# A fused retention layer and channel-mix layer: two blocks in 64-token chunks, and a new order of all pieces

## Chip, cores and metric

The kernel runs on one core of one Trainium2 chip. The metric is device microseconds of one launch. The time before is 153.07 us, the median of three runs (153.02 to 153.23).

## What is computed

```python
# attention: q, k, v of shape (4, 8, 768, 64); per head a decay gamma
for t in range(S):
    state = gamma * state + outer(k[t], v[t])       # 64 x 64
    y[t] = q[t] @ state / sqrt(D)
x = y.transpose(0, 2, 1, 3).reshape(4, 768, 512)
# channel mix: d_model 512, d_ff 1024
x_prev = x shifted by one token (zero first)
xk = mu_k * x + (1 - mu_k) * x_prev
xr = mu_r * x + (1 - mu_r) * x_prev
k = maximum(xk @ w_k, 0);  v = (k * k) @ w_v
out = sigmoid(xr @ w_r) * v
```

The output is float32; the kernel multiplies in float16 and sums in float32.

## The kernel before

The 4 x 768 tokens are cut into 12 blocks of 256 tokens; blocks 0 to 2 are the first sequence, 3 to 5 the second, and so on. The recurrence is done in chunks: inside a chunk by masked scores (queries times keys) times values, across chunks by a state of 64 x 64 per head, with the decay folded into scale factors of v and of the result. A block is done in one of three forms. Blocks 0 and 1 use chunks of 128 tokens made of even and odd tokens. Blocks in `WIDE` (2 to 5) use two plain chunks of 128 tokens with score tiles of 128 x 128. Blocks in `HALF` (6 to 11) use four chunks of 64 tokens with score tiles of 64 x 64, so that TensorE works on four 64x64 tiles; these have more, smaller matmuls and one mask instruction instead of two, but four running states instead of two. The transposes of blocks 0 to 3 (`WHOLE`) read 128 rows, those of the others 64.

Nothing is scheduled automatically. `ORDER` is a text that lists every piece of the program; the loop at its end issues the pieces in that order, each to the engine behind the `~` (v VectorE, a ScalarE, p GpSimd's queue, s SyncE's queue; none is TensorE), with the PSUM banks behind the `@`. Each engine works through its own queue strictly in this order; semaphores for the data are set automatically. The codes, with the block as the first number:

- `lq`, `lk`, `lv`: loads of q, k, v (float32 in memory; q and k land as float16); `wk`, `wr`, `wv`: weights. Their issues stand in GpSimd's queue (lines 230, 235, 735, 738, 742).
- `Tq`, `Tk`: transposes (272, 278); `Eq`, `Ek`: their copies to `qT`, `kT` on ScalarE (241).
- `vs`: scaling of v (253), mostly VectorE, for blocks 1 and 3 GpSimd.
- `S`: scores (318 in the 64-token form, 331 wide, 339 the first form); `M`: mask (347, 354).
- `C`: state of the chunk (366 in the 64-token form, 384, 395); `U`: running state sums (419); `G`: decay to the next block, on ScalarE 4 instructions (424).
- `I`, `J`: state times queries (441); `Y`: masked scores times values (462 in the 64-token form, 478 wide, 489), in the 64-token form with `J` inside it.
- `D`: scaled result to `xT` (507, 514); `dx`: difference of neighbouring tokens (529); `t`: the same role for block 0 on ScalarE (542); `X.n.0.j`, `X.n.1.j`: mixed inputs xk and xr of block n, column chunk j of four (552, 558).
- `K`: xk @ w_k (582; 572 for pairs of blocks that share a group); `Qa`, `Qb`: relu and square on ScalarE (591, 599, 603); `R`: xr @ w_r (612); `s`: its sigmoid (618); `V`: times w_v (624; `Vc` in halves 642); `O`: product (630, 649); `st`: store (637).
- `z`: matmuls of zeros (703, 710), which fill TensorE's waiting time at the start.

The dense pieces `K`, `R`, `V` need all column chunks of the mixed inputs of their group; a group is one block or a pair (`GROUPS`: 3 with 4, 6 with 7, 9 with 10).

Of the kernel before, what the change touches and what calls it, by code (L numbers as in the profile page):

```python
# [48 lines left out]
X.3.1.2~v I.6@01 J.5 X.3.1.0~v D.5~v X.3.1.1~v Qb.3.3~a G.6~a V.2.1.0@2 K.3.1@3 V.2.1.1 O.2.1~v  # L49
Qb.3.7~a Qa.3.1~a Qb.3.1~a dx.5~v K.3.4@4 K.3.5@5 Qa.3.5~a X.5.0.0~v X.5.0.3~v R.3.1@2 s.3.1~a  # L50
lv.7~p Qa.3.4~a X.5.0.1~v Qb.3.4~a R.3.0@5 R.4.0@2 s.3.0~a s.4.0~a Qb.3.0~a X.5.0.2~v vs.7~v K.5.2@4
S.7@67 st.1.1~s M.7~v Qb.3.5~a Y.6 Qb.3.6~a lv.10~p C.7@23 U.7.0~v X.5.1.1~v Qa.5.2~a K.5.0@5
R.4.1@6 Qa.5.0~a D.6~v s.4.1~a V.4.0.0@4 V.4.0.1 V.3.1.0@5 U.7.1~v Qb.5.0~a X.5.1.3~v U.7.2~v I.7@01
X.5.1.2~v U.7.3~v Tq.8@67 Eq.8~a X.5.1.0~v O.4.0~v lv.8~p vs.8~v Qb.5.2~a lq.10~p lk.8~p Tk.8@23
Ek.8~a V.3.1.1 V.3.0.0@4 C.8@67 O.3.1~v st.2.1~s st.3.1~s Y.7 dx.6~v D.7~v Tq.10@23 V.3.0.1 Eq.10~a
G.7~a dx.7~v X.6.0.2~v V.4.1.0@5 R.5.1@2 s.5.1~a K.5.3@0 Qa.5.3~a R.5.0@2 U.8.0~v O.3.0~v V.4.1.1
lv.9~p lk.10~p lq.9~p Tk.10@01 s.5.0~a U.8.1~v X.6.0.1~v Ek.10~a X.6.0.0~v Tk.9@23 Ek.9~a K.5.1@7
Qa.5.1~a X.6.0.3~v K.6.0@4 lq.11~p Qb.5.1~a Qa.6.0~a U.8.2~v I.8@01 vs.9~v S.8@23 M.8~v O.4.1~v
st.4.1~s K.6.4@7 Qa.6.4~a vs.10~v X.6.1.2~v K.6.2@6 C.9@23 Qa.6.2~a Qb.6.2~a U.9.0~a Y.8 U.9.1~v
D.8~v U.9.2~v U.9.3~v X.6.1.3~v Qb.5.3~a Tq.9@45 V.5.1.0@6 V.5.1.1 O.5.1~v Eq.9~a lk.11~p K.6.3@7  # L60
Qa.6.3~a K.6.7@4 Qa.6.7~a V.5.0.0@7 C.10@45 Qb.6.0~a X.6.1.0~v S.9@23 M.9~v G.9~a Qb.6.3~a Tq.11@01
Eq.11~a V.5.0.1 dx.8~v X.6.1.1~v st.4.0~s K.6.1@6 Qb.6.7~a Qa.6.1~a Qb.6.1~a X.8.0.3~v X.8.0.0~v
U.10.0~v U.10.1~v K.6.5@2 Qa.6.5~a st.3.0~s lv.11~s K.6.6@0 Qa.6.6~a Qb.6.6~a R.6.0@6 s.6.0~a
O.5.0~v U.10.2~v U.10.3~v R.7.0@2 s.7.0~a R.6.1@7 s.6.1~a I.9@45 X.8.0.2~v S.10@23 Tk.11@01 Ek.11~a
X.8.0.1~v K.8.1@7 Qb.6.5~a Qa.8.1~a Qb.8.1~a vs.11~v st.5.1~s K.8.0@6 C.11@01 M.10~v Qb.6.4~a
X.8.1.0~v X.8.1.2~v Y.9 D.9~v G.10~a U.11.0~v st.5.0~s U.11.1~v U.11.2~v Qa.8.0~a I.10@23 V.6.1.0@7
V.6.1.1 O.6.1~v V.6.0.0@4 V.6.0.1 I.11@01 S.11@67 M.11~v dx.9~v V.7.1.0@5 V.7.1.1 Y.10 D.10~v
dx.10~v X.9.0.3~v X.9.0.0~v Y.11 Qb.8.0~a X.9.0.2~v R.7.1@6 s.7.1~a X.9.0.1~v V.7.0.0@7 V.7.0.1
K.8.3@6 O.7.0~v X.9.1.0~v D.11~v X.8.1.1~v Qa.8.3~a Qb.8.3~a K.8.2@2 Qa.8.2~a Qb.8.2~a X.8.1.3~v
dx.11~v X.11.1.0~v X.11.1.1~v X.9.1.1~v V.8.1.0@6 K.9.2@3 X.11.0.0~v K.9.6@7 Qa.9.6~a V.8.1.1  # L70
Qa.9.2~a Qb.9.2~a X.11.0.3~v K.9.5@7 K.9.3@3 K.9.0@2 Qa.9.0~a Qb.9.6~a V.8.0.0@0 V.8.0.1 Qb.9.0~a
Qa.9.5~a Qb.9.5~a Qa.9.3~a O.7.1~v st.7.1~s X.9.1.2~v X.11.0.1~v O.6.0~v K.9.7@1 R.8.1@7 s.8.1~a
K.9.1@5 R.8.0@7 X.9.1.3~v X.11.0.2~v st.6.1~s O.8.1~v R.9.1@4 R.9.0@6 K.11.0@3 K.11.3@2 s.8.0~a
Qa.9.1~a Qb.9.1~a Qb.9.3~a V.10.0.0@5 V.9.0.0@7 Qa.11.0~a Qb.11.0~a Qa.11.3~a s.9.0~a K.9.4@6
R.10.0@2 Qa.9.7~a X.11.1.3~v st.6.0~s K.11.1@1 Qa.11.1~a Qa.9.4~a K.11.2@3 Qb.9.7~a Qb.9.4~a
Qa.11.2~a X.11.1.2~v O.8.0~v st.7.0~s st.8.1~s st.8.0~s V.9.1.0@1 V.10.1.0@6 s.10.0~a V.9.1.1
# [723 lines left out]
```

## Time and profile before

| | |
|---|---|
| median of three runs | 153.07 us |
| profiled execution | 153.06 us, span 151.3 us |
| TensorE matmul busy | 143.5 us (95%), 2426 instructions |
| VectorE busy | 127.5 us (84%), 212 instructions |
| ScalarE busy | 103.4 us (68%), 195 instructions |
| GpSimd busy | 55.3 us (37%), 65 instructions |
| granted TensorE clock | 1.00 in all stretches |
| TensorE busy from 45 to 105 us | 60.0 of 60.0 us |

Busy shares are means over stages. What matters for an order is where TensorE stands idle, and what ended the wait; the timeline prints this in square brackets behind an instruction.

### The profile page before, as it was taken

The numbers are of one execution on the slowest core, as the hardware profiler recorded it, in microseconds if no ns is written. First come the engines' busy times: TensorE is split into PE (matmuls) and PEld (weight loads), VectorE is DVE, ScalarE is ACT, GpSimd is POOL, SyncE is SP. The second block draws the span as 40 slices with busy tenths as digits, with TensorE's granted clock in tenths as the row PEclk, the third lists the DMA queues.
The fourth block names the chain that finished last, engine by engine and source line by source line (L and its number), as shares of the span: only waits on it lengthen the run. The fifth ranks groups of instructions, "written<-read, shape, count | busy, mean of one in ns | idle before, by whom it ended". The sixth has DMA issues, their size and how long they took to land.

```text
span 151.3 us, 5540 instructions
## 1 busy us (share of the span) xinstructions
PE 143.5 (95%) x2426; PEld 82.9 (55%) x2426; DVE 127.5 (84%) x212; ACT 103.4 (68%) x195; POOL 55.3 (37%) x65
## 2 busy tenths in 40 slices
...
GB/s 126 235 230 194 208 228 195 167 247 215 196 166 203 233 260 119 269 289 197 230 172 122 6 45 281 100 41 39 0 4 0 4 0 215 201 0 0 153 129 139
DMA packets 45624, 22.16 MB, mean 146 GB/s; under 512 B 37400, under 2 KB 41248, under 8 KB 45600
## 3 DMA queue, kind: packets, MB, share of 16 engines
...
q8 instruction: 19, 0.31, 0.8%
...
## 4 chain that ended last, share of the span: by engine, by line
PE 86%; ACT 3%; DVE 3%; POOL 2%; DMA 2%; issue 1%; SPq 0%; DVEq 0%
PE ps L624 27%; PE ps L612 14%; PE ps L572 14%; PE ps L582 13%; PE ps L278 3%; PE ps L441 2%; DMA k2s<-in_k_dram 2%; PE ps L272 2%; DVE a L354 2%; PE ps L478 1%; ACT qT L241 1%; POOL vs L253 1%; PE ps L366 1%; PE ps L462 1%; PE ps L642 1%; POOL k L230 1%
## 5 line engine op out<-in xcount | busy, mean ns | idle before, releaser
L624 PE MATMUL ps<-wv,k2s 128*128 128x512 f16 x184 | 44.1, 380 | 0.0
L591 ACT ACTIVATE kr<-ps 128x512 f32<-128x512 f32 x48 | 27.8, 593 | 12.6 <-PE ps L582 6.6
L624 PEld LDWEIGHTS <-k2s 128*128 128x128 f16 x184 | 17.1, 98 | 18.9 <-ACT k2s L603 0.4
L630 DVE SCALAR_TENSOR_TENSOR os<-ps,rs 128x512 f32<-128x512 f32 x23 | 15.7, 684 | 11.9 <-ACT rs L618 9.4
L612 PE MATMUL ps<-wr,xr 128*128 128x512 f16 x96 | 23.5, 379 | 0.0
L582 PE MATMUL ps<-xk,wk 128*128 128x256 f16 x192 | 23.2, 273 | 0.0
L572 PE MATMUL ps<-xk,wk 128*128 128x512 f16 x96 | 23.0, 379 | 0.0
L618 ACT ACTIVATE rs<-ps 128x512 f32<-128x512 f32 x24 | 13.6, 597 | 12.9 <-PE ps L612 12.1
L230 POOL DMA_DIRECT2D k<-in_k_dram x20 | 17.7, 902 | 10.1 <-PE ps L384 6.8
L582 PEld LDWEIGHTS <-wk 128*128 128x128 f16 x192 | 18.1, 98 | 3.7
L241 ACT COPY qT<-ps 128x1024 f16<-128x1024 f16 (+1 forms) x13 | 12.3, 946 | 9.2 <-PE ps L278 7.8
L558 DVE SCALAR_TENSOR_TENSOR xr<-dx,mu,xT 128x256 f16<-128x256 f32 (+1 forms) x32 | 17.9, 577 | 0.1
L230 POOL DMA_DIRECT2D v<-in_v_dram x18 | 16.0, 911 | 3.9 <-DVE a L354 2.2
L558 DVE SCALAR_TENSOR_TENSOR xk<-dx,mu,xT 128x256 f16<-128x256 f32 (+1 forms) x32 | 17.0, 579 | 0.2
L354 DVE TENSOR_TENSOR a<-ps,c_sb 128x1024 f16<-128x1024 f32 (+1 forms) x14 | 14.6, 1066 | 0.7 <-PE ps L339 0.4
L603 ACT ACTIVATE k2s<-kr 128x512 f16<-128x512 f32 x24 | 14.8, 631 | 0.3
L612 PEld LDWEIGHTS <-xr 128*128 128x128 f16 x96 | 9.1, 98 | 10.7 <-issue 0.5
L572 PEld LDWEIGHTS <-wk 128*128 128x128 f16 x96 | 9.1, 98 | 10.5
L599 ACT ACTIVATE k2s<-kr 128x512 f16<-128x512 f32 x24 | 14.5, 627 | 0.3
L529 DVE TENSOR_TENSOR dx<-xT 128x1024 f32<-128x1024 f32 x11 | 13.4, 1222 | 0.2
L241 ACT COPY kT<-ps 128x1024 f16<-128x1024 f16 (+1 forms) x13 | 12.2, 944 | 1.9 <-PE ps L272 1.4
L253 DVE TENSOR_TENSOR vs<-v,csm_sb 128x1024 f16<-128x1024 f32 x10 | 12.2, 1217 | 0.0
...
## 6 DMA issues: line engine op xcount, KB each, us to landing
...
```

Of the source, the lines that this page charges most:

```text
L230: e.dma_start(out=dst[:, :, i * D : i * D + D], in_=src[:, i * P : i * P + P].rearrange("h p d -> p h d"),)
L241: e.copy(out=out, in_=in_)
L354: nc.vector.tensor_tensor(out=a_full(n)[:, i, :, j0:j1], in0=pairs(banks("S", n, i, j0))[:, :, j0:j1], in1=(below if wide(n) else causal[: ...
L558: nc.vector.scalar_tensor_tensor(out=XM[w](k)[:, j, t0:t1], in0=DX(k)[:, j, t0:t1], scalar=mu[:, w * NCO + j : w * NCO + j + 1], in1=x[:, ...
L572: nc.tensor.matmul(banks("K", n, g), lhsT=wk16[:, co, g * P : g * P + P], rhs=XM[0](k)[:, co, :], start=(co == 0), stop=(co == NCO - 1),)
L582: nc.tensor.matmul(pz[:, i, :], lhsT=wk16[:, co, fo * P : fo * P + P], rhs=XM[0](k)[:, co, m * TM + t0 : m * TM + t1], start=(i == 0 and c ...
L591: nc.scalar.activation(out=kr, in_=banks("K", n, g, *u), func=AF.Relu)
L599: nc.scalar.activation(out=k2s[:, n % 3 : n % 3 + 2, g, :], in_=kr, func=AF.Square,)
L603: nc.scalar.activation(out=K2(n)[:, w * g : w * g + w, t0:t1], in_=kr.rearrange("p a t -> p (a t)").rearrange("p (i t) -> p i t", i=w), fu ...
L612: nc.tensor.matmul(banks("R", n, tb), lhsT=XM[1](k)[:, co, t : t + P], rhs=wr16[:, co, :], start=(co == 0), stop=(co == NCO - 1),)
L624: nc.tensor.matmul(banks("V", n, tb), lhsT=K2(n)[:, fo, tb * P : tb * P + P], rhs=wv16[:, fo, :], start=(fo == 0), stop=(fo == NFO - 1),)
L630: nc.vector.scalar_tensor_tensor(out=OS(2 * n + tb), in0=banks("V", n, tb), scalar=1.0 / (KSC * KSC), in1=RS(2 * n + tb), op0=ALU.mult, op ...
```

## The change

Blocks 4 and 5 move from the list of wide blocks to that of the 64-token chunks. Their scores become 32 matmuls of 64x64 each, their masks one instruction instead of two, their running states four (three for block 5, the last of its sequence) instead of two, and their `J` becomes part of `Y`. The text of the order is new from the first scores of block 1 on: the loads of block 3 (k, q, v) come ahead of `wr` and of those of block 4, the decays of blocks 6, 9 and 10 run on VectorE instead of ScalarE, there are two runs of zero matmuls (2 and 3) instead of three of 2, and nearly every piece has another place and other banks. No function is changed. Of the order, the beginning and the end are shown:

```diff
--- before.py
+++ after.py
 KSC = 64.0
 KUP = 4.0
-HALF = (6, 7, 8, 9, 10, 11)
+HALF = (4, 5, 6, 7, 8, 9, 10, 11)
 EARLY = ((1, 0, 0), (0, 0, 0))
 GROUPS = ((0,), (1,), (2,), (3, 4), (5,), (6, 7), (8,), (9, 10), (11,))
 APART = (0,)
 WHOLE = (0, 1, 2, 3)
-WIDE = (2, 3, 4, 5)
+WIDE = (2, 3)
 HEADS = ((0, 1), (3, 2), (4, 5), (7, 6))
...
 lk.0.2.4~p Tk.0.2.4@3 Ek.0.2.4~a lq.0.2.4~p vs.0~v C.0@67 U.0.0~v Tq.0.2.4@2 Eq.0.2.4~a lq.1~p
 lk.1~p M.0.1.0.2~v z.2@3 S.0.1.2.4@23 U.0.1~v lv.1~p lk.2~p I.0@01 S.0.0.2.4@67 M.0.0.2.4~v wk.0~p
 wk.1~p G.0~a z.2@6 Tq.1@6 Eq.1~a vs.1~p lq.2~p Tk.1@7 Ek.1~a M.0.0.0.2~v M.0.1.2.4~v Y.0 D.0~v
-t.0.0.3~a t.0.0.2~a t.0.0.1~a lv.2~p z.2@4 S.1.1@23 M.1.1~v C.1@01 U.1.0~v z.2@4 I.1@23 S.1.0@67
-X.0.0.1~v t.0.1.2~a X.0.0.2~v Tk.2@0 t.0.1.3~a t.0.0.0~a M.1.0~v X.0.0.0~v z.2@4 Y.1 t.0.1.1~a
-X.0.0.3~v Ek.2~a K.0.0@0 K.0.1@6 lq.4~p U.1.1~v G.1~a wr~p lk.4~p D.1~v dx.1~v X.1.0.2~v X.1.0.0~v
-K.0.2@1 Qa.0.0~a Qb.0.0~a Qa.0.2~a lq.3~p X.1.0.1~v X.1.0.3~v X.1.1.0~v Qa.0.1~a K.0.3@0 Qa.0.3~a
-lk.3~p vs.2~v Tq.2@1 X.1.1.2~v K.1.3@6 K.1.0@0 C.2@7 U.2.0~v lv.3~p Eq.2~a S.2.1@23 M.2.1~v S.2.0@45
-M.2.0~v Qb.0.3~a lv.4~p K.1.1@1 X.1.1.1~v Qa.1.0~a t.0.1.0~a K.1.2@7 I.2@23 Qb.0.1~a Qa.1.1~a wv.0~p
-Qb.0.2~a Tq.4@01 Eq.4~a Y.2 Qa.1.3~a Qb.1.1~a X.0.1.3~v X.1.1.3~v R.1.1@4 Tk.4@01 Ek.4~a J.2 R.1.0@6
-Qa.1.2~a s.1.0~a X.0.1.2~v X.0.1.1~v X.0.1.0~v R.0.1@5 s.0.1~a s.1.1~a R.0.0@7 s.0.0~a S.4.1@01
-Qb.1.0~a D.2~v dx.2~v X.2.0.2~v X.2.0.0~v S.4.0@23 Tq.3@4 Eq.3~a X.2.0.1~v wv.1~p X.2.0.3~v Tk.3@7
-lq.5~p Ek.3~a K.2.2@5 Qa.2.2~a K.2.3@4 M.4.1~v M.4.0~v Qa.2.3~a Qb.2.3~a lk.6~p S.3.1@67 M.3.1~v
-S.3.0@01 vs.3~p C.3@23 U.3.0~a Qb.2.2~a K.2.1@4 Qa.2.1~a K.2.0@2 Qa.2.0~a I.3@45 lq.6~p vs.4~v
-C.4@67 U.3.1~v X.2.1.1~v V.0.1.0@3 M.3.0~v V.1.0.0@2 G.3~a U.4.0~v I.4@01 X.2.1.3~v U.4.1~v J.3
-Qb.1.3~a Y.4 Qb.2.0~a lk.5~p X.2.1.2~v X.2.1.0~v Y.3 D.3~v dx.3~v V.0.0.0@7 V.0.1.1 O.0.1~v Tq.5@45
-J.4 D.4~v dx.4~v R.2.0@6 Qb.2.1~a V.0.0.1 O.0.0~v X.3.0.1~v Eq.5~a Qb.1.2~a V.1.0.1 X.3.0.2~v
-O.1.0~v Tq.6@01 Eq.6~a Tk.6@45 Ek.6~a st.0.0~s lk.7~p st.1.0~s V.1.1.0@3 V.1.1.1 O.1.1~v s.2.0~a
-R.2.1@0 s.2.1~a lv.5~p X.3.0.0~v X.3.0.3~v Tk.7@67 Ek.7~a G.4~a S.6@45 M.6~v Tk.5@23 Ek.5~a vs.5~v
-V.2.0.0@0 K.3.2@1 Qa.3.2~a K.3.0@6 S.5.0@23 M.5.0~v S.5.1@45 C.5@1 U.5.0~v K.3.3@7 Qb.3.2~a Qa.3.0~a
-lq.7~p K.3.7@6 Qa.3.3~a Qa.3.7~a lv.6~p lq.8~p vs.6~v M.5.1~v V.2.0.1 st.0.1~s I.5@67 O.2.0~v
-st.2.0~s C.6@23 U.6.0~a U.6.1~v U.6.2~v K.3.6@1 Qa.3.6~a lk.9~p X.3.1.3~v Y.5 Tq.7@45 Eq.7~a U.6.3~v
...
-O.9.0~v R.11.1@4 V.10.1.1 Qb.11.1~a V.11.0.0@7 R.11.0@5 s.11.0~a st.9.0~s Vc.11.1.1@1 s.11.1~a
-O.10.1~v st.10.1~s Oc.11.1.1~v V.11.0.1 O.11.0~v st.11.0~s sc.11.1.1~a Vc.11.1.0@4 Oc.11.1.0~v
+t.0.0.3~a t.0.0.2~a t.0.0.1~a lv.2~p t.0.1.1~a z.2@4 S.1.1@23 M.1.1~v X.0.0.2~v t.0.0.0~a Tk.2@7
+t.0.1.0~a Ek.2~a t.0.1.2~a C.1@01 U.1.0~v lk.3~p z.3@4 I.1@23 X.0.0.1~v S.1.0@45 t.0.1.3~a X.0.0.0~v
+X.0.0.3~v K.0.0@0 M.1.0~v Y.1 U.1.1~v X.0.1.2~v K.0.3@1 G.1~a K.0.1@4 lq.3~p X.0.1.0~v Qa.0.3~a
+Qb.0.3~a Qa.0.1~a D.1~v dx.1~v Tq.2@1 Eq.2~a K.0.2@2 Qa.0.2~a Qa.0.0~a Qb.0.0~a S.2.1@45 S.2.0@67
+X.0.1.1~v X.1.0.3~v X.1.0.0~v X.1.0.1~v X.1.0.2~v K.1.3@2 Qa.1.3~a X.1.1.2~v Tk.3@0 X.1.1.0~v
+X.0.1.3~v vs.2~v M.2.0~v K.1.1@1 Ek.3~a Qa.1.1~a Tq.3@2 Eq.3~a C.2@0 U.2.0~v M.2.1~v K.1.0@3
+S.3.1@01 M.3.1~v S.3.0@67 M.3.0~v Qb.0.2~a K.1.2@2 I.2@45 lv.3~p wr~p Qb.0.1~a X.1.1.3~v lq.4~p
+lk.4~p Y.2 lv.4~p vs.3~p C.3@01 Qa.1.2~a Qb.1.2~a R.0.0@2 U.3.0~a Qa.1.0~a U.3.1~v G.3~a X.1.1.1~v
+I.3@01 Qb.1.3~a J.2 D.2~v dx.2~v X.2.0.0~v X.2.0.1~v s.0.0~a X.2.0.2~v X.2.0.3~v R.1.0@3 Y.3 s.1.0~a
+Tq.4@45 Eq.4~a J.3 D.3~v Tk.4@67 vs.4~v dx.3~v R.0.1@3 s.0.1~a R.1.1@4 K.2.1@5 Ek.4~a K.2.2@3
+K.2.0@2 Qa.2.2~a wv.0~p S.4@01 Qa.2.1~a Qb.2.2~a Qa.2.0~a X.2.1.2~v M.4~v X.2.1.0~v C.4@67 U.4.0~v
+U.4.1~v U.4.2~v V.0.0.0@5 s.1.1~a K.2.3@2 V.0.1.0@4 wv.1~p V.0.1.1 Qb.1.0~a I.4@01 Qa.2.3~a Qb.1.1~a
+V.1.0.0@6 X.2.1.3~v O.0.1~v U.4.3~v G.4~a Qb.2.3~a st.0.1~s lv.5~p vs.5~v V.0.0.1 O.0.0~v X.2.1.1~v
+V.1.0.1 O.1.0~v lk.5~p C.5@45 lk.6~p Tk.5@23 Y.4 R.2.0@6 s.2.0~a Ek.5~a U.5.0~v U.5.1~v D.4~v
+R.2.1@5 V.1.1.0@6 V.1.1.1 U.5.2~v dx.4~v X.3.0.3~v O.1.1~v Tk.6@23 X.3.0.2~v Qb.2.1~a s.2.1~a
+Qb.2.0~a lq.7~p Tq.7@45 Eq.7~a lq.5~p Tq.5@01 Eq.5~a X.3.0.1~v X.3.1.2~v V.2.1.0@7 V.2.1.1 V.2.0.0@6
+O.2.1~v I.5@01 X.3.0.0~v S.5@45 Ek.6~a lq.6~p Tq.6@23 V.2.0.1 lv.6~p vs.6~v Eq.6~a K.3.1@7 Qa.3.1~a
+Qb.3.1~a M.5~v K.3.0@2 K.3.4@7 K.3.2@3 Qa.3.4~a Qb.3.4~a Qa.3.2~a Qa.3.0~a Y.5 C.6@45 U.6.0~a
+Qb.3.2~a K.3.6@7 Qa.3.6~a X.3.1.3~v X.3.1.1~v X.3.1.0~v R.4.1@2 Qb.3.6~a s.4.1~a K.3.7@3 lv.7~p
+vs.7~v D.5~v st.0.0~s st.2.1~s O.2.0~v Qa.3.7~a Qb.3.7~a lk.7~p R.4.0@6 s.4.0~a U.6.1~v dx.5~v
+X.5.0.0~v S.6@01 U.6.2~v Tk.7@23 X.5.0.1~v M.6~v Ek.7~a R.3.1@7 s.3.1~a K.3.3@4 Qa.3.3~a K.3.5@2
+Qa.3.5~a I.6@01 C.7@67 U.6.3~v X.5.0.2~v G.6~v Qb.3.5~a X.5.0.3~v U.7.0~v U.7.1~v S.7@45 Qb.3.3~a
+U.7.2~v lv.9~p lv.8~p K.5.3@2 Qa.5.3~a lq.10~p K.5.1@3 M.7~v Qb.3.0~a lk.8~p Qa.5.1~a R.3.0@6
...
+st.8.1~s V.9.1.1 st.8.0~s O.9.0~v s.10.0~a V.10.0.0@6 V.10.0.1 Qb.11.3~a Qb.11.2~a Vc.11.1.1@1
+R.10.1@0 O.9.1~v V.10.1.1 s.11.1~a st.9.1~s O.10.0~v s.10.1~a O.10.1~v st.9.0~s st.10.1~s
+Oc.11.1.1~v V.11.0.1 st.10.0~s s.11.0~a O.11.0~v st.11.0~s sc.11.1.1~a Vc.11.1.0@2 Oc.11.1.0~v
 sc.11.1.0~s
 """
 
```

More of the change, by code (lines that the diff above doesn't have):

```diff
@@ L47 @@
-lq.7~p K.3.7@6 Qa.3.3~a Qa.3.7~a lv.6~p lq.8~p vs.6~v M.5.1~v V.2.0.1 st.0.1~s I.5@67 O.2.0~v
-st.2.0~s C.6@23 U.6.0~a U.6.1~v U.6.2~v K.3.6@1 Qa.3.6~a lk.9~p X.3.1.3~v Y.5 Tq.7@45 Eq.7~a U.6.3~v
[L49 to L76, printed above, removed]
@@ L77 @@
-V.10.0.1 s.9.1~a O.9.1~v st.9.1~s Qb.11.2~a Qb.11.3~a O.10.0~v st.10.0~s R.10.1@4 V.9.0.1 s.10.1~a
-O.9.0~v R.11.1@4 V.10.1.1 Qb.11.1~a V.11.0.0@7 R.11.0@5 s.11.0~a st.9.0~s Vc.11.1.1@1 s.11.1~a
-O.10.1~v st.10.1~s Oc.11.1.1~v V.11.0.1 O.11.0~v st.11.0~s sc.11.1.1~a Vc.11.1.0@4 Oc.11.1.0~v
+t.0.0.3~a t.0.0.2~a t.0.0.1~a lv.2~p t.0.1.1~a z.2@4 S.1.1@23 M.1.1~v X.0.0.2~v t.0.0.0~a Tk.2@7
+t.0.1.0~a Ek.2~a t.0.1.2~a C.1@01 U.1.0~v lk.3~p z.3@4 I.1@23 X.0.0.1~v S.1.0@45 t.0.1.3~a X.0.0.0~v
+X.0.0.3~v K.0.0@0 M.1.0~v Y.1 U.1.1~v X.0.1.2~v K.0.3@1 G.1~a K.0.1@4 lq.3~p X.0.1.0~v Qa.0.3~a
@@ new lines @@
+Qa.3.5~a I.6@01 C.7@67 U.6.3~v X.5.0.2~v G.6~v Qb.3.5~a X.5.0.3~v U.7.0~v U.7.1~v S.7@45 Qb.3.3~a
+U.7.2~v lv.9~p lv.8~p K.5.3@2 Qa.5.3~a lq.10~p K.5.1@3 M.7~v Qb.3.0~a lk.8~p Qa.5.1~a R.3.0@6
+s.3.0~a I.7@45 U.7.3~v X.5.1.2~v X.5.1.1~v X.5.1.0~v lk.9~p Tk.8@23 Ek.8~a Y.6 D.6~v lv.10~p K.5.2@6
+Qa.5.2~a dx.6~v V.4.1.0@2 V.4.1.1 O.4.1~v V.3.0.0@0 G.7~a K.5.0@1 Qa.5.0~a Qb.5.0~a vs.8~v Y.7 D.7~v
+Qb.5.1~a dx.7~v lq.8~p Tq.8@23 X.6.0.2~v X.6.0.1~v X.6.0.0~v Tk.9@67 Ek.9~a V.3.0.1 V.4.0.0@1
+st.2.0~s st.1.0~s V.3.1.0@4 V.3.1.1 V.4.0.1 X.6.0.3~v O.4.0~v C.8@67 U.8.0~v Eq.8~a U.8.1~v U.8.2~v
```

20 lines of the change are left out of this document (added).

## Prediction

> **What bounds the kernel now.** I read the page first, then the busy time by stretches, then the chain of work that ended last in order of time, and last the timelines of each engine between 15 and 50 us, because there the order changes first.
>
> ```profile
> span 151.3 us, 5540 instructions
> ```
>
> The profiled execution took 153.06 us: 151.3 us of span and 1.8 us around it. The median of the three runs is 153.07 us, so sums against this execution need no correction. By stretches (after the stretch: its length, then busy time of TensorE, its weight loads, VectorE, ScalarE, GpSimd):
>
> ```profile
> 15.00:45.00 30.00, 28.77 (x538) 20.35 (x527) 29.34 (x46) 25.53 (x50) 23.98 (x28) 1.00 1.55 203
> 45.00:105.00 60.00, 60.00 (x1310) 32.99 (x1309) 58.94 (x89) 46.48 (x85) 21.09 (x24) 1.00 1.04 165
> ```
>
> Two engines are full at once. TensorE has no gap from 45 to 105 us, and VectorE is busy for 98% of 15 to 105 us. The order is written by hand, each engine runs its queue strictly in that order, and so the time is: TensorE's own work plus every moment at which it stands before a piece whose input is not there. Only one such moment of size is left after 20 us, at the state of block 3 (C.3), which waits for GpSimd's scaled values:
>
> ```profile
> 37.76 0.44 PE L384 MATMUL ps<-vs,k 128*64 128x64 f16 x16 [0.26 <-POOL vs L253]
> ```
>
> The pieces of TensorE come from the chain (start, duration, what):
>
> ```profile
> 18.79 0.64 PE ps L489 x32
> ...
> 19.54 3.60 PE ps L582 x32
> 23.14 0.57 PE ps L272 x16
> ...
> 25.89 0.55 PE ps L331 x16
> ...
> 40.29 0.37 PE ps L384 x16
> ...
> 59.33 0.24 PE ps L441 x8
> ...
> 60.79 0.57 PE ps L478 x16
> ...
> 87.00 0.26 PE ps L441 x16
> ...
> 89.73 0.29 PE ps L462 x28
> ...
> 94.93 0.38 PE ps L366 x32
> 95.31 0.27 PE ps L318 x32
> ...
> 95.84 0.97 PE ps L624 x4
> 96.81 2.59 PE ps L572 x12
> ```
>
> A dense piece (K, R or V) takes 2.59 / 3 = 0.86 us; the K of blocks 0 to 2 take 3.60 / 4 = 0.90. The first dense piece after attention work takes 0.97, and the first small piece after a dense one takes 0.38 where the same kind inside a visit takes 0.27. So one visit to attention work among dense work costs about 0.11 + 0.11 = 0.2 us beyond its pieces.
>
> **Part 1: blocks 4 and 5 in 64-token chunks (TensorE).** Scores: 16 matmuls of 64x128 (L331, 0.55) become 32 of 64x64 (L318, 0.27): -0.28 per block. Scores times values: 16 at L478 (0.57) become 32 at L462 (28 in 0.29, so 0.33): -0.24 per block. State: 16 at L384 (0.37) become 32 at L366 (0.38, as the first of a visit both): 0. Inter-chunk: two sets of 8 at L441 become two of 16; as first of a visit 0.24 against 0.26: 0. Two blocks: 2 x 0.52 = -1.0 us. The count of TensorE matmuls grows by 128 here.
>
> [...] In the rows 32 matmuls of 64x64 take 0.27 us, 8.4 ns each, because four tiles work side by side. [...]
>
> **Part 2: the order (TensorE).** From the first K piece on the old order has 25 visits to attention work, the new one 28: 3 x 0.22 = +0.66. Inside visits the old one changes between 128-row and 64x64 tiles eight times, the new one twice; no row isolates that change, so I bound its six removals between 0 and the 0.11 of entering a visit (-0.66) and take the middle, -0.3. One zero matmul fewer and another place of Tk.2 only move filling work ahead of the first K. TensorE's work: -1.0 + 0.66 - 0.3 = -0.7 us, bounds -1.1 and -0.3.
>
> **Part 3: VectorE, ScalarE.** Per block one mask less (1.14), two state sums more (2 x 0.33), and the decay of blocks 6, 9 and 10 comes from ScalarE to VectorE (taken like a state sum of the same size, 0.33 each): -2.3 + 1.3 + 1.0 = 0. VectorE stays as full as it is; ScalarE gets lighter. Neither moves the sum, but where the new order places the pieces does.
>
> **Part 4: walking the new order.** The rows for it: VectorE's start times, ScalarE's, GpSimd's scaling, and loads with issue and landing.
>
> ```profile
> 15.26 1.22 DVE L354 TENSOR_TENSOR a<-ps,c_sb 128x1024 f16<-128x1024 f32 x1
> 16.40 0.41 DVE L419 TENSOR_TENSOR tg<-ps,tg 128x256 f16<-128x256 f32 x1
> 16.73 0.87 DVE L552 SCALAR_TENSOR_TENSOR xk<-xT,mu,dx 128x256 f16<-128x256 f32 x2
> ...
> 19.77 1.22 DVE L514 TENSOR_TENSOR xT<-ps,gy_sb 128x1024 f32<-128x1024 f32 x1
> 21.02 1.22 DVE L529 TENSOR_TENSOR dx<-xT 128x1024 f32<-128x1024 f32 x1
> 22.28 1.68 DVE L558 SCALAR_TENSOR_TENSOR xk<-dx,mu,xT 128x256 f16<-128x256 f32 x4
> ```
> ```profile
> 20.86 0.58 ACT L591 ACTIVATE kr<-ps 128x512 f32<-128x512 f32 x1
> 21.47 0.63 ACT L603 ACTIVATE k2s<-kr 128x512 f16<-128x512 f32 x1
> ...
> 23.75 1.03 ACT L241 COPY qT<-ps 128x1024 f16<-128x1024 f16 x1
> ```
> ```profile
> 35.79 1.92 POOL L253 TENSOR_TENSOR vs<-v,csm_sb 128x1024 f16<-128x1024 f32 x1
> ```
>
> From start to start a mask takes 1.14, a state sum 0.33, a mix (X) 0.40, yout (D) 1.25, differ (dx) 1.26.
>
> *First K and Y.1.* The mask M.1.1 starts at 15.26 as before. Behind it stand four X, one U and M.1.0: 16.40 + 4 x 0.40 + 0.33 + 1.14 = 19.5. Y.1 then runs to 19.6 + 0.75 = 20.35 (18.79 to 19.54 in the rows), with K.0.0 done under M.1.0. Before, Y.1 and the first K were done at 19.54 + 0.90 = 20.44. Gain 0.1.
>
> *S.2 waits for Eq.2.* TensorE: 20.35 + K.0.3, K.0.1 1.80 + Tq.2 0.57 + K.0.2 0.90 = 23.6. ScalarE has Qa.0.3, Qb.0.3 and Qa.0.1 ahead of the copy Eq.2: from K.0.3's end at 21.3, 0.61 + 0.6 + 0.5 + 1.03 = 24.0. Wait 0.4.
>
> *K.1.3 waits for X.1.0.2.* VectorE after M.1.0: U 0.33, two X 0.80, D.1 1.25, dx.1 1.26, five X 2.0: 19.5 + 5.6 = 25.1, visible at 25.2. TensorE comes to the piece at 24.0 + 0.55 and to its third column chunk 0.22 later, 24.8. Wait 0.4; the end is at 25.85.
>
> *C.3 and R.0.0 wait for loads.* TensorE then has Tk.3, K.1.1, Tq.3, C.2, K.1.0, S.3, K.1.2, I.2, Y.2: 0.57 + 0.9 + 0.57 + 0.3 + 0.9 + 0.55 + 0.9 + 0.24 + 0.57 = 5.5, so it comes to C.3 at 31.3. The new order puts the loads of block 3 (k, q, v) ahead of wr and of block 4's q and k. In this trace the loads land one after another:
>
> ```profile
> L230 POOL DMA_DIRECT2D v<-in_v_dram x2: 907/912/917, 16.2 to 17.1; - x2
> ...
> DMA to landing us min/median/max: 7.0/7.0/7.1
> ```
> ```profile
> L235 POOL DMA_DIRECT2D q<-in_q_dram x1: 929/929/929, 18.0 to 18.0; - x1
> ...
> DMA to landing us min/median/max: 7.4/7.4/7.4
> ```
> ```profile
> L738 POOL DMA_DIRECT2D wr<-in_moe_w_r_dram x1: 823/823/823, 18.8 to 18.8; - x1
> ...
> DMA to landing us min/median/max: 9.3/9.3/9.3
> ```
> ```profile
> L230 POOL DMA_DIRECT2D v<-in_v_dram x1: 889/889/889, 25.6 to 25.6; - x1
> ...
> DMA to landing us min/median/max: 10.1/10.1/10.1
> ```
>
> Block 2's v has landed at 24.2, block 4's q at 25.4, wr at 28.1 (so wr takes 2.7), block 3's v last at 35.7. The set between 24.2 and 35.7 is the same in both orders: 11.5 us, wr 2.7, and eight others of 1.1 each. In the new order: two k, q, two v of block 3 by 24.2 + 5 x 1.1 = 29.7, wr at 32.4, block 4's k at 35.7. GpSimd's scaling vs.3 stands behind the issue of block 4's loads, waits for its v, and runs 29.7 + 1.9 = 31.6; the issue of wv stands behind it and has time. So C.3 waits 0.3 and ends at 32.0, and R.0.0, the first piece to read wr, waits 0.4 to 0.5. Tk.4 comes at 35.6 and finds block 4's k just landed. If the loads go 10% faster both waits vanish; 10% slower, they sum to 1.5.
>
> *Later.* K.2.1 needs X.2.0.3 at 37.9 only for its fourth chunk. From there to X.5.0.3 VectorE's queue is 3 D, 3 dx, 3 masks, 4 value scalings, 8 short and 8 long X, 10 U, 6 results, 1 decay:
>
> ```profile
> 49.29 0.68 DVE L630 SCALAR_TENSOR_TENSOR os<-ps,rs 128x512 f32<-128x512 f32 x1
> 49.89 1.40 DVE L558 SCALAR_TENSOR_TENSOR xk<-dx,mu,xT 128x512 f16<-128x512 f32 x2
> 51.22 1.28 DVE L630 SCALAR_TENSOR_TENSOR os<-ps,rs 128x512 f32<-128x512 f32 x2
> ...
> 54.87 1.21 DVE L253 TENSOR_TENSOR vs<-v,csm_sb 128x1024 f16<-128x1024 f32 x1
> ```
>
> With 0.60 for a result, 0.67 for a long X and 1.14 for a scaling that is 31.4 us: 69.3. TensorE's own pieces bring it to K.5.3, which needs X.5.0, at about 69.4: no wait, but no slack. Behind that VectorE runs ahead by 1 us and more in the new order as in the old, and the last pieces (V.11.0.1, then the last half of block 11) are the same.
>
> **Sum.** -0.1 start, -0.7 work, +1.6 waits (0.4 + 0.4 + 0.3 + 0.5), -0.3 for the wait at C.3 that was there before: +0.5, so 153.06 + 0.5, said as **153.5 us**. The bounds of work (-1.1 to -0.3) and of waits (0.8 to 2.3) give its own range 152.7 to 154.6 with all on one side, mostly 153.2 to 153.9.
>
> **Rivals.**
> 1. *Waits hidden, only the work counts (not slower).* Place: C.3 and R.0.0. Block 3's k and q land earlier; if the queue of loads has v by 29.3 and wr by 31.9, both waits vanish: 153.06 - 0.1 - 0.7 - 0.3 + 0.8 = 152.8, and with one of the other two waits gone as well 152.4; with the bound of -1.1, 152.0. For it: every wait computed is under 0.6 us. Against: the loads land steadily, and wr's place is three loads later. Chance 0.20.
> 2. *VectorE becomes the bound at 60 to 75 us.* It is 98% busy and has nothing in reserve at K.5.3. Each result piece (O) that VectorE must take in order waits for its V; if those and D.2 to D.5, which wait for the late R.0.0 and J.2, leave it idle for over 0.1 us in all, every further 0.1 us is paid again by TensorE at K.5.3. With 0.6 to 1.4 us: 154.1 to 154.9. Chance 0.28.
> 3. *Small matmuls do not overlap.* If each cost what a 64x128 one does, 0.55 / 16 = 34 ns, the 128 more cost +4.4 instead of -1.0: 158.9. [...] Chance 0.02.
>
> **How the numbers follow.** My forecast has 0.50. A change under 0.2% (0.31 us, about what a measurement of this kernel can tell) reaches to 153.38; a third of my case lies below that (0.17 same, 0.33 slower). Rival 1 gives 0.17 faster and 0.03 same; rivals 2 and 3 are slower. Faster 0.17, same 0.20, slower 0.63. Range 152.4 to 154.8: it leaves out the lower half of rival 1, the tip of rival 2 and rival 3.
>
> **What would show it.** In the new profile: L331 and L478 at 32 matmuls each instead of 64, L318 at 256 in pieces of 0.27; idle TensorE of 0.4 before S.2 (released by ScalarE's qT) and inside K.1.3 (VectorE's xk), then before C.3 (GpSimd vs, near 31.5) and R.0.0 (the load of wr, near 32.4). Wrong would be: no idle time there, wr landed before 31.9, a gap before K.5.3 near 69 us, or a first K plus Y.1 not done by 20.4.

## Result and the profile after

The changed kernel takes 158.88 us (median of six runs, 157.17 to 160.79) against 153.16 us; the ratio is 1.031 (95% interval 1.026 to 1.036). The ratio leaves out the two longest of the six runs, 160.38 and 160.79 us, as slow ones. The forecast was 153.5 us with a range up to 154.8: the sign was the likelier one, the size was far too small. The profiled execution of the changed kernel took 158.77 us, 5.71 more than that of the kernel before.

From the page, and from the busy time by stretches (columns as in the prediction):

```profile
span 157.0 us, 5779 instructions
PE 144.4 (92%) x2553; PEld 82.9 (53%) x2553; DVE 128.6 (82%) x219; ACT 100.9 (64%) x183; POOL 55.3 (35%) x65
q8 instruction: 20, 0.33, 0.9%
```
```profile
15.00:45.00 30.00, 26.58 (x538) 18.94 (x538) 28.88 (x44) 24.22 (x48) 24.88 (x28) 1.00 1.53 214
45.00:105.00 60.00, 57.67 (x1300) 31.12 (x1297) 55.44 (x88) 43.65 (x76) 20.67 (x24) 1.00 1.01 155
```

TensorE, without a gap from 45 to 105 us before, now stands idle there for 2.3 us, and VectorE has more idle time as well: neither became the bound. The timeline of TensorE shows where it stands (start, duration, what, and in brackets the idle time ahead and what ended it):

```profile
20.88 1.92 PE L582 MATMUL ps<-xk,wk 128*128 128x256 f16 x16
...
24.66 0.62 PE L331 MATMUL ps<-qT,kT 64*128 64x128 f16 x16 [0.32 <-ACT qT L241]
25.22 1.28 PE L582 MATMUL ps<-xk,wk 128*128 128x256 f16 x8
...
31.96 0.42 PE L384 MATMUL ps<-vs,k 128*64 128x64 f16 x16
32.31 1.04 PE L612 MATMUL ps<-wr,xr 128*128 128x512 f16 x4
33.60 0.41 PE L441 MATMUL ps<-qT,tg 64*64 64x128 f16 x12 [0.25 <-DVE t L419]
...
37.64 0.22 PE L278 MATMUL ps<-c_sb,k 64*64 64x64 f16 x2 [1.38 <-issue]
...
50.51 1.25 PE L612 MATMUL ps<-wr,xr 128*128 128x512 f16 x5
52.70 0.81 PE L612 MATMUL ps<-wr,xr 128*128 128x512 f16 x3 [0.93 <-issue]
...
58.76 0.28 PE L441 MATMUL ps<-qT,tg 64*64 64x64 f16 x9
59.82 0.24 PE L441 MATMUL ps<-qT,tg 64*64 64x64 f16 x5 [0.78 <-issue]
...
76.39 0.26 PE L278 MATMUL ps<-c_sb,k 64*64 64x64 f16 x9
77.26 0.38 PE L278 MATMUL ps<-c_sb,k 64*64 64x64 f16 x23 [0.62 <-issue]
```

The four large stops have no data behind them. Each falls inside a piece: 30 transposes of Tk.4 run, then 1.38 us nothing, then the last two; R.2.0 and R.2.1 are eight matmuls in a row, and the stop is behind the fifth, the first of R.2.1. The releaser is "issue": nothing that the profile shows. From matmul start to matmul start, less the usual step, the four take 1.6, 1.1, 0.95 and 0.8 us, 4.4 in all.

Counted over all matmuls of the trace, the stops stand before the matmuls number 607, 862, 990 and 1374: 94 or 95 modulo 128. A matmul comes with one weight load (2553 of each), so 128 of them are 256 instructions. The page has a queue of 16 KB packets, "instruction" (q8), with 20 packets of 0.33 MB in all for 2553 matmuls (19 and 0.31 MB for 2426 in the kernel before), about one for each 128 pairs; by estimate that is 64 bytes an instruction, from 16 KB and 256 instructions. The view of the DMA queues, cut to the stretches around the last packet ahead of the stops at 52.7 and 77.3 us, shows it:

```profile
q0 software_dynamic: 319, 0.36, 111.6%
q1 hardware_dynamic: 15, 0.03, 7.9%
q8 instruction: 1, 0.02, 5.3%
```
```profile
q0 software_dynamic: 779, 0.12, 149.5%
q1 hardware_dynamic: 63, 0.10, 28.2%
q8 instruction: 1, 0.02, 5.4%
```

These are 49.8 to 51.3 and 75.0 to 76.1 us. By the single packets, they run from 49.90 to 51.18 and from 75.04 to 75.98, among the packets of the loads, and TensorE goes on 1.5 and 1.3 us behind their landing. So the trace shows blocks of 16 KB, a queue of their own, and the fetch of one block while the one before it runs: the blocks that run during these two fetches begin at 46.59 and 71.09 us. The four stops cost 4.4 of 158.8 us.

What a block needs follows from the single packets. In the four cases the fetch of the next block starts 3.3 to 4.3 us after TensorE has executed the first matmul of the present one, takes 0.9 to 1.3, and TensorE resumes 1.3 to 1.5 after the landing: 6.0 to 7.1 us in all. The 128 pairs of those blocks, without the stop itself, took 4.4 to 6.2 us. In the kernel before, the tightest block behind 20 us (70.82 to 78.15 us) took 7.3 and needed 7.0. A dense pair takes 0.11 or 0.21 us (0.86 us for eight or four), a small one 0.008 (0.27 for 32), so a block that holds several attention pieces is used up fast.

The rest of the 5.7 us: 0.95 lies behind TensorE's end. Its last matmuls and SyncE's stores from their start on, before:

```profile
147.05 1.04 PE L642 MATMUL ps<-wv,k2s 128*128 128x256 f16 x8
147.97 0.33 SPq L637 DMA_DIRECT2D out_dram<-os  x1
148.58 0.33 SPq L657 DMA_DIRECT2D out_dram<-os  x1
```

and in the changed kernel:

```profile
151.81 1.04 PE L642 MATMUL ps<-wv,k2s 128*128 128x256 f16 x8
151.93 1.30 SPq L637 DMA_DIRECT2D out_dram<-os  x3
153.34 0.69 SPq L657 DMA_DIRECT2D out_dram<-os  x1
```

From TensorE's end to the end of the span it was 151.3 - 148.1 = 3.2 us and is 157.0 - 152.85 = 4.15: st.9.0 and st.10.0 stand in SyncE's queue behind later tiles' stores, and all come at the end: three stores and the last half in place of one and the last half. Last, TensorE's end is 4.76 us later, 0.3 more than the stops. In this execution the first transposes start at 6.47 in place of 6.07, the first scores at 8.53 in place of 7.88, and the mask M.1.1, where the orders part, at 15.88 in place of 15.26, in a part of the program that is the same in both: 0.6 late from there on. This start varies from execution to execution: over the traces of both orders with the same start, M.1.1 begins between 15.2 and 15.9 us. The waits and the work behind it come to about -0.3.

### The profile page after: what moved, and what is told of

Same layout as the page of the kernel before. It is cut to its first block, busy times and chain, and to the rows that moved or that the text cites. A ratio compares the mean times of both kernels' runs of the same rounds, so it can differ in the third digit from the quotient of the medians.

```text
span 157.0 us, 5779 instructions
## 1 busy us (share of the span) xinstructions
PE 144.4 (92%) x2553; PEld 82.9 (53%) x2553; DVE 128.6 (82%) x219; ACT 100.9 (64%) x183; POOL 55.3 (35%) x65
## 4 chain that ended last, share of the span: by engine, by line
PE 80%; DVE 11%; issue 4%; ACT 2%
PE ps L624 26%; PE ps L572 14%; PE ps L612 13%; PE ps L582 9%; PE ps L703 3%; DVE a L354 3%; PE ps L278 3%; PE ps L441 2%; PE ps L318 2%; PE ps L462 2%; PE ps L366 1%; PE ps L272 1%; ACT qT L241 1%; PE ps L642 1%; DVE xk L552 1%
## 5 line engine op out<-in xcount | busy, mean ns | idle before, releaser
L624 PE MATMUL ps<-wv,k2s 128*128 128x512 f16 x184 | 43.4, 379 | 0.0
L612 PE MATMUL ps<-wr,xr 128*128 128x512 f16 x96 | 24.5, 379 | 0.9 <-issue 0.9
L582 PE MATMUL ps<-xk,wk 128*128 128x256 f16 x192 | 24.2, 273 | 0.3 <-DVE xk L552 0.3
L582 PEld LDWEIGHTS <-wk 128*128 128x128 f16 x192 | 18.0, 98 | 5.1 <-issue 0.8
L558 DVE SCALAR_TENSOR_TENSOR xr<-dx,mu,xT 128x256 f16<-128x256 f32 (+1 forms) x32 | 17.4, 577 | 0.0
L235 POOL DMA_DIRECT2D q<-in_q_dram x12 | 10.8, 905 | 9.0 <-PE ps L278 5.8
L507 DVE TENSOR_TENSOR xT<-ps,gy_sb 128x512 f32<-128x512 f32 x16 | 11.0, 689 | 2.7 <-PE ps L441 1.0
```

What stands on the lines that cost most here:

```text
L558: nc.vector.scalar_tensor_tensor(out=XM[w](k)[:, j, t0:t1], in0=DX(k)[:, j, t0:t1], scalar=mu[:, w * NCO + j : w * NCO + j + 1], in1=x[:, ...
L582: nc.tensor.matmul(pz[:, i, :], lhsT=wk16[:, co, fo * P : fo * P + P], rhs=XM[0](k)[:, co, m * TM + t0 : m * TM + t1], start=(i == 0 and c ...
L612: nc.tensor.matmul(banks("R", n, tb), lhsT=XM[1](k)[:, co, t : t + P], rhs=wr16[:, co, :], start=(co == 0), stop=(co == NCO - 1),)
L624: nc.tensor.matmul(banks("V", n, tb), lhsT=K2(n)[:, fo, tb * P : tb * P + P], rhs=wv16[:, fo, :], start=(fo == 0), stop=(fo == NFO - 1),)
```

## Experiments

Theory A: TensorE's program comes in blocks of 128 pairs, late while loads run; what decides is which pieces stand between the borders. Theory B: the stops come from the order itself or from waits that the profile doesn't show.

### First set: each half alone, and borders moved by small matmuls

**e3**: the order of before, blocks 4 and 5 in 64-token chunks.

```diff
-HALF = (6, 7, 8, 9, 10, 11)
+HALF = (4, 5, 6, 7, 8, 9, 10, 11)
-WIDE = (2, 3, 4, 5)
+WIDE = (2, 3)
-... S.5.0@23 M.5.0~v S.5.1@45 C.5@1 U.5.0~v ...
+... S.5@23 M.5~v C.5@45 U.5.0~v U.5.1~v U.5.2~v ...
```

> The kernel before in its own order, with blocks 4 and 5 in 64-token chunks alone (each two scores and two masks become one, the state sums four and three, the second inter-chunk part moves into the values of the scores, which therefore stand a little later). By the prediction's part 1 this is worth -1.0 us of TensorE's work and the waits of the new order are absent: 152.0 to 153.0. Theory A: the 128 added pairs fall into the time of the loads, borders move by up to 128 pairs between 33 and 65 us; one or two stops of about 1 us each: 153 to 155.

Measured: 159.48 us (158.71 to 160.67), ratio 1.040 (1.032 to 1.048).

**e4**: the new order, blocks 4 and 5 wide (the reverse edit in the changed kernel, their J again pieces of their own).

> The changed kernel's order with blocks 4 and 5 wide as before (two scores and two masks each, two state sums and one, the inter-chunk part by itself). By the prediction: the data waits of the new order without its gain, 154 to 155.5. Theory A: 128 pairs fewer between 40 and 65 us, so the stops there (near 52 and 59 us) shrink or vanish, while those before block 4 and behind block 5 stay (near 37 and 77 us): 155 to 157. If the order's data waits were the whole loss, it would stay at 157 to 160.

Measured: 161.1 us (159.59 to 162.27, the longest being the profiled one), ratio 1.046 (1.037 to 1.056). The prediction's numbers for the halves, 152 to 153 and 154 to 155.5, are both far off: each half alone costs about as much as both together or more. Theory A's ranges, up to 155 and 157, were too low as well. Their main stops:

```profile
56.48 0.48 PE L278 MATMUL ps<-c_sb,k 64*64 64x64 f16 x20 [2.50 <-issue]
56.90 1.89 PE L624 MATMUL ps<-wv,k2s 128*128 128x512 f16 x4
```
```profile
37.16 0.22 PE L278 MATMUL ps<-c_sb,k 64*64 64x64 f16 x2 [0.97 <-issue]
57.70 0.41 PE L278 MATMUL ps<-c_sb,q 64*64 64x64 f16 x27 [1.43 <-issue]
80.76 0.38 PE L278 MATMUL ps<-c_sb,k 64*64 64x64 f16 x23 [1.57 <-issue]
```

The first fence is of e3, the second of e4. All stand at numbers that are 94 or 95 modulo 128 again; e4 has 128 matmuls fewer than the changed kernel and still stops. The stops aren't the whole loss. In e3, the granted clock behind the stop of 2.50 us is 0.52 from 56.2 to 59.6 us, and the four matmuls of the second row take 1.89 us, where four of this kind take 1.04 elsewhere; by 3.4 x 0.48 that is an estimate of 1.6 us more. TensorE also waits there for data: 0.76 at 43 us, 0.60 at 65 and 0.37 at 67. In e4 it waits 1.01 at 44 us.

**e1, e2**: 48 or 32 more pairs ahead, as 64x64 matmuls of zeros.

```diff
-... ck.0.0.2~a cq.0.0.2~a z.12@6
+... ck.0.0.2~a cq.0.0.2~a z.8@6 zt.50@6        (e1: kernel before; e2: zt.34 in the changed one)
```

> The kernel before, with 48 more matmul and weight-load pairs on TensorE: 50 matmuls of 64x64 on zeros stand behind the first zero matmuls (two of these instead of three), in time that TensorE spends waiting for the first loads. Nothing else changes. Theory A (instruction blocks): TensorE's instructions come in blocks of 128 pairs by transfers that queue with the loads; the 48 pairs move every block border 48 pairs earlier in the work, so that blocks with much attention work end before the next block is there: stops without a data cause near 57 us and 80 us, in all 3 to 6 us, time 156 to 159. Theory B (the new kernel is slower by waits for data that its order makes): these pairs change no order and no data, time 153.0 to 153.5.

> The changed kernel, with 32 more pairs put in at the same place. Theory A: the stops, now at pairs 607, 862, 990 and 1374 from the start, are again at pairs 94 + 128 k of the kernel's own count, which are other pieces of the order; with the borders 32 pairs earlier more time is lost (2 to 4 us more): 160 to 163, and no stop stays at the piece where it was (Tk.4, R.2.1, I.5, Tk.8). Theory B: the stops stay at the same pieces, time 158 to 160.

Measured: e1 164.1 us (162.59 to 185.44; ratio 1.066, 1.056 to 1.076), e2 158.41 (157.64 to 161.70; 1.034, 1.025 to 1.042). e1 lost more than A said, and its profiled execution, the one of 185.44, ran at a granted clock of 0.765, so its trace says nothing. e2's time is what B said. In its profiled run, the longest of five, the stops are at other pieces (46.9 us in L366, 78.7 us in L582), as A has it, but the first K starts at 21.67 us in place of 18.67: the edit also took away one of the three large zero matmuls of the start. Neither is a clean control.

### Second set: the borders alone

The same columns of zeros in more matmuls: nothing else changes, not even the work.

```diff
 for _ in range(count // 4):          # float32, 512 columns; count % 4: float16
-    nc.tensor.matmul(pz, lhsT=zero, rhs=zero[:, None, :].to_broadcast([P, 4, P]), ...)
+    for a in range(4):               # in the first n of them
+        nc.tensor.matmul(pz[:, a * P : (a + 1) * P], lhsT=zero, rhs=zero, ...)
```

> The kernel before, in which one of the three float32 zero matmuls at the start (512 columns) is four of 128 columns: the same columns, 6 more pairs of weight load and matmul in TensorE's program, everything behind them moved by 6 pairs. Theory A (TensorE's program comes in blocks of 128 pairs by a DMA queue of its own, and TensorE stops where a block isn't there yet): in the kernel before, the blocks landed at least 1.7 us ahead of the first pair of the next block, and a border moved by 6 pairs costs nothing: 153.0 to 153.6 us. Theory B (the stops come from the order of the pieces or from the waits between engines, not from the place of the borders): the same, 153.0 to 153.5 us. Together with the run of 24 pairs it shows that the edit itself costs nothing.

> The kernel before, in which the three float32 zero matmuls at the start and two of the float16 ones (512 columns) are four of 128 columns each: the same columns and the same work, 24 more pairs in TensorE's program ahead of all else; no other edit. Theory A: the borders of the blocks now fall 24 pairs earlier in the work, where the kernel before had 1.7 to 2 us to spare at five of them between 20 and 95 us; a model of the landings from the traces gives stops of 0.5, 0.6, 0.9, 2.1 and 0.9 us: 156.5 to 159 us, with stops in the middle of pieces that nothing but the issue releases. Theory B: 153.0 to 153.8 us, and no such stops.

> The changed kernel with two of the float32 zero matmuls at the start in four pieces each: the same work and order, 12 more pairs ahead. Theory A: the borders move, and by the same model the stops come to 2.9 us in place of 4.6: 156.5 to 158.3 us, the stops at other places within the pieces (12 pairs earlier in the work). Theory B: as the changed kernel, 158.4 to 159.4 us, with stops at the same places.

Measured: f1 153.39 us (ratio 0.9996, 0.997 to 1.002), f2 156.44 (1.0185, 1.012 to 1.025), f3 156.59. Six pairs at the start cost nothing, 24 cost 3.3 us, and 12 in the changed kernel save 2.3. In the profiled runs, TensorE's idle time by "issue" falls from 3.7 us in the changed kernel to 1.9 in f3, and f3's M.1.1 starts 0.7 earlier, so its 2.3 are not the borders alone. In f2 a piece of the kernel before stops in its middle, and TensorE stops again between two pieces:

```profile
76.15 0.39 PE L278 MATMUL ps<-c_sb,k 64*64 64x64 f16 x24
77.90 0.26 PE L278 MATMUL ps<-c_sb,k 64*64 64x64 f16 x8 [1.37 <-issue]
...
84.37 1.02 PE L612 MATMUL ps<-wr,xr 128*128 128x512 f16 x4 [1.50 <-issue]
```

In the kernel before the first of these pieces is one row of 32:

```profile
75.85 0.45 PE L278 MATMUL ps<-c_sb,k 64*64 64x64 f16 x32
```

There the same border falls 24 pairs further on, at 78.15 us inside a later piece, and TensorE doesn't stop. B is out: order, work and waits are the same in both.

### Third set: without the loads

```diff
 def go(e, n, j0=0, j1=NJ):
+    if n >= 6:
+        return
     b, t0 = n // NB, n % NB * TM
```

> The changed kernel without the loads of q, k and v of blocks 6 to 11 (their pieces work on what blocks 2 to 5 left in the same tiles); all other instructions stay. Theory A: the blocks of TensorE's program then meet no queue of loads behind about 50 us: the stop near 37 us stays (0.8 to 1.5 us), the three at 52.7, 59.8 and 77.3 us (2.3 us by idle, 2.9 us with what else was late) go, and a fetch starts 1 to 2.5 us after TensorE's front has come into the block before: 155.5 to 157 us. Theory B: the stops stay where they are: 158 to 159.5 us.

> The changed kernel without the loads of q, k and v of blocks 6 to 11, once more for its trace. Theory A: the stop near 37 us stays (0.8 to 1.5 us), the three at 52.7, 59.8 and 77.3 us are gone; 154.9 to 156.2 us. Theory B: stops at the same three places.

> The kernel before without the loads of q, k and v of blocks 6 to 11, the counterpart of the changed kernel without them (155.7 us). Theory A: the kernel before has no stops to lose, so it gains nothing, or as much as its waits for late v are worth (0 to 0.5 us): 152.5 to 153.3 us; and the two kernels without these loads differ by the stop at 37 us (1.4 us), the end of the span (0.9 us) and the prediction's 0.4 us: 2.3 to 3 us in place of 5.7. Theory B: both gain alike, and the difference stays at 5 to 6 us.

> The kernel before with the 24 more pairs at the start (156.44 us) and without the loads of q, k and v of blocks 6 to 11. Theory A (a block of the program comes late because its fetch waits among the loads): the stops of 0.5, 1.4 and 1.5 us at 56, 78 and 84 us go, 0.2 to 0.6 us near 20 us stay: 153.2 to 154.2 us. Theory B (the place of a border costs by itself, with loads or without): 156 to 156.8 us.

Measured: f4 155.72 us, g1 155.49 (two runs; the profiled one 154.40), g2 153.49, h3 153.81. The profiled execution of f4 took 284 us, so g1 was run for the trace; f4's other nine took 154.3 to 156.1. The kernel before gains nothing without the loads, with 24 more pairs it falls from 156.44 to 153.81, and the changed kernel falls by 3.2. The groups of TensorE's instructions by line (busy time, mean, and behind the second bar the idle time and its releaser), first of the changed kernel, then of g1, whose lines are two further down:

```profile
L612 PE MATMUL ps<-wr,xr 128*128 128x512 f16 x96 | 24.5, 379 | 0.9 <-issue 0.9
L441 PE MATMUL ps<-qT,tg 64*64 64x64 f16 (+1 forms) x288 | 7.6, 201 | 1.4 <-issue 0.8 <-DVE tg L419 0.4 <-DVE t L419 0.2
L278 PE MATMUL ps<-c_sb,k 64*64 64x64 f16 x256 | 4.1, 195 | 2.0 <-issue 2.0
```
```profile
L614 PE MATMUL ps<-wr,xr 128*128 128x512 f16 x96 | 24.4, 380 | 0.0
L443 PE MATMUL ps<-qT,tg 64*64 64x64 f16 (+1 forms) x288 | 7.4, 201 | 0.6 <-DVE tg L421 0.4 <-DVE t L421 0.2
L280 PE MATMUL ps<-c_sb,k 64*64 64x64 f16 x256 | 3.7, 195 | 0.0
```

In g1 no stop is left, and behind 44 us a fetch starts -1.4 to 1.4 us after the first matmul of the block, in place of 3.3 to 4.3. That the stop at 37 us would stay was a miss: it is gone in g1 (its block landed at 34.40 in place of 36.15) and comes back in two later runs without these loads, with 0.45 and 1.24 us. In h3 the stop near 20 us stays, with 0.44 at 22.0, and those at 56, 78 and 84 us are gone, as A has it.

### What is left without the stops

**h4**: e3 without the loads.

> The order of before with blocks 4 and 5 in 64-token chunks and 64x64 tiles (159.48 us with all loads), without the loads of q, k and v of blocks 6 to 11. By the prediction's first part the chunks save 0.7 to 1.0 us of TensorE's work: without stops 152.4 to 153.2 us, against 153.49 us of the kernel before without these loads. If the smaller pieces wait for their sums on VectorE (0.8 us idle near 43 us with all loads): 153.5 to 155 us.

Measured: 155.12 us (154.47 to 156.77), above g2's 153.49. No issue stop is left; the 64-token sums come late in an order made for the wide form:

```profile
43.67 0.43 PE L443 MATMUL ps<-qT,tg 64*64 64x64 f16 x18 [0.68 <-DVE tg L421]
```

Two more waits that g2 doesn't have follow: 0.32 at 61 us for the scaled v of VectorE, and 0.37 at 63 us for a relu of ScalarE.

**h1, h2**: two stores at the place where their products are done, in f3 and in f4's kernel.

```diff
-... O.9.0~v s.10.0~a ... O.10.0~v s.10.1~a O.10.1~v st.9.0~s st.10.1~s Oc.11.1.1~v V.11.0.1 st.10.0~s ...
+... O.9.0~v st.9.0~s s.10.0~a ... O.10.0~v st.10.0~s s.10.1~a O.10.1~v st.10.1~s Oc.11.1.1~v V.11.0.1 ...
```

> The changed kernel with the 12 more pairs at the start (156.59 us), and in SyncE's queue two stores taken out of the pile at the end: st.9.0 ahead of st.9.1 and st.10.0 ahead of st.10.1, each right behind its product; nothing else moves. If the pile of stores is what makes the span end 0.95 us later behind TensorE's last matmul than in the kernel before, the time falls by 0.6 to 1.0 us: 155.6 to 156.0 us. If not: 156.4 to 156.8 us.

> The changed kernel without the loads of q, k and v of blocks 6 to 11 (their pieces work on what earlier blocks left), and with the two stores out of the pile. With neither stops nor pile it should show the prediction's own sum: 0.5 us over the kernel before without these loads (153.49 us): 153.6 to 154.6 us. If the loss lies elsewhere (the granted clock, waits of TensorE that were not counted): 155 us or more.

Measured: h1 156.84 us (155.63 to 157.01; f3 156.59), h2 154.75 (153.29 to 156.03; f4 155.72). From TensorE's end to the span's end it is 155.1 - 151.64 = 3.46 us in h1 and 154.8 - 150.62 = 4.18 in f3, so the pile was worth 0.7 us in the trace; the medians show it only in h2. The runs of both lie in two groups, h2's at 153.3 to 153.7 and 154.4 to 155.3, with one at 156.0. In the profiled run of the upper group, TensorE waits for the second half of wk ahead of K.0.3:

```profile
21.38 1.92 PE L584 MATMUL ps<-xk,wk 128*128 128x256 f16 x16 [1.03 <-DMA wk<-in_moe_w_k_dram]
```

It landed at 20.36 in the changed kernel's trace, where K.0.3 came at 20.88, and at 21.33 here.

**i1, i2**: h1 and h2 with K.0.1, which needs only the first half, ahead of K.0.3.

```diff
-... K.0.3@1 G.1~a K.0.1@4 ... Qa.0.3~a Qb.0.3~a Qa.0.1~a ...
+... K.0.1@1 G.1~a K.0.3@4 ... Qa.0.1~a Qa.0.3~a Qb.0.3~a ...
```

> As h1 (the changed kernel with 12 more pairs at the start and the two stores earlier; 155.6 to 157.0 us), and K.0.1, which reads the first half of wk, ahead of K.0.3, which reads the second (their banks and relus change places with them). The second half lands between 19.9 and 21.3 us in the traces and K.0.3 came to it at 20.2 to 20.4; now it comes 0.9 us later, as in the kernel before. If that wait makes the upper group of h1's runs: 155.5 to 156.1 us and a smaller spread. If the groups come from stops: no change, 155.6 to 157.0 us.

> As h2 (the changed kernel without the loads of q, k and v of blocks 6 to 11, whose pieces work on what earlier blocks left, and with the two stores earlier; 154.75 us, in two groups), and K.0.1 ahead of K.0.3. If the wait for the second half of wk makes the upper group: 153.3 to 153.9 us in one group, within 0.5 us of the kernel before without these loads (153.49 us). If not: two groups as before, 154.5 to 155 us.

Measured: i1 156.33 us (156.16 to 157.31), i2 154.53 (154.45 to 155.20). No wait for wk is left (in i1 it landed at 21.48), but i2 stays at 154.5: its profiled run has a stop of 1.24 us at 36.9 and waits 0.70 ahead of S.2. So the wait for wk makes part of the spread and isn't the whole of it; what separates h2's groups isn't settled.

**g3, g4** missed their aim. g3 put the product of tile 11.0 ahead of the store of tile 9.0, whose buffer it takes, so that the rows of tile 9.0 get those of 11.0, and the store stayed in the pile. In g4, Eq.2 ahead of Qa.0.1, the second half of wk came 0.91 late, and S.2 then waited 0.62.

> The changed kernel with the 12 more pairs at the start (156.59 us), and with the last output tile but one earlier: V.11.0.1 ahead of R.10.1, and its product and store ahead of those of tile 10.1, so that VectorE's last four operations and the last stores are spread as in the kernel before. If the stores that pile up behind each other at the end cost the 0.95 us that the span's end comes later behind TensorE's end, the time falls by 0.5 to 0.9 us: 155.7 to 156.1 us. If the last store takes that long for another reason, it stays within 0.2 us of 156.6.

> The changed kernel with the 12 more pairs at the start (156.59 us), and on ScalarE the copy Eq.2 ahead of the relu Qa.0.1, for which the score piece S.2 waits 0.32 us. By the prediction (a wait of TensorE there is paid in full at the end) the wait goes and the time falls by 0.2 to 0.3 us: 156.2 to 156.4 us, unless the stops behind it move too. If the wait is taken back by what TensorE has to wait for later: 156.5 to 156.7 us.

Measured: 156.42 (155.49 to 157.12) and 157.15 us (156.93 to 157.62), against f3's 156.59. They tell nothing on the pile or on the price of the wait at S.2. None of the versions beats the kernel before.

## Why the prediction was wrong

- **The failed step** is the first: "the time is: TensorE's own work plus every moment at which it stands before a piece whose input is not there". The instructions are an input too. The prediction counted 128 more matmuls by what they take to execute, and nothing by what it takes to bring them; in the profiled run 4.4 us of 5.7 are that. The number of matmuls isn't what decides: e4 has none of the 128 and stops as well. What decides is how fast TensorE uses up each block while the loads run: ahead of the four stops in 4.4 to 6.2 us, where the next block needed 6.0 to 7.1. That the kernel before has no such stop hangs on where its borders fall: 24 more pairs at the start undo it.
- **Part 1** held in its rows: a score piece of 32 takes 0.27 to 0.28 us (69.36 to 69.64 us). But no run shows the gain of 1.0 us. From the first K to TensorE's last matmul, h4 takes 130.60 us with 2.24 of idle time and g2, its counterpart without the 64-token chunks, 129.12 with 0.70: 128.4 of work in both. Where the gain went stays open.
- **Rival 3**: its 158.9 is the measured time by chance, since 32 matmuls take 0.27 us together and not 32 x 34 ns.
- **Part 2 and the sum without stops**: from M.1.1's start to TensorE's last matmul it is 132.8 us in the kernel before and 137.0 in the changed one, 132.5 of them without the stops. Without the loads it is 133.3 in g2 and 132.6 in g1's profiled run, which has no stop. So work and waits come to -0.3 and -0.7, where the sum said +0.5; that is near rival 1's 152.8. That the forecast had the right sign is luck: the time rose by the stops and the pile, which are not in the sum. g1's trace is one run of 154.40 us, and most runs of f4 took longer; h2's lower group, at 153.3 to 153.7, fits it, but no trace of that group was taken. A slip in the working: with all terms on the low side the sum gives 152.4, not 152.7.
- **Part 4**: S.2 waits 0.32 for Eq.2 (0.4 predicted); K.1.3 is 0.23 longer than a piece without a wait (1.28 against 1.05; 0.4 predicted). C.3 and R.0.0 don't wait: v of block 3 landed at 29.2 and wr at 31.6, the "10% faster" of the text, so this part went as rival 1. A wait of 0.25 at I.3 for VectorE was not in the walk. "First K and Y.1 by 20.35" was right by its sum (K.0.3 at 20.88 with the start 0.65 late), but that K.0.3 reads the half of wk that lands at 20.0 to 21.5 was overlooked: it waits 0.5 to 1.0 us for it in four of the traces (g3, g4, h1, h2).
- **Rival 2** did not come: TensorE has no idle time ahead of K.5.3, and VectorE is idler than before from 45 to 105 us.
- **"The last pieces are the same"** was said of TensorE; the order of the stores was not walked, and cost 0.95 us.
